# Half-block scores, outputs one pair late, and a split quadrant stretch in a fused attention and FFN kernel

## The chip, the cores and the metric

The kernel runs on one core of a Trainium2 chip. The metric is the device time of one execution in microseconds (us), lower is better. Times of a kernel are given as the median of several runs. "Faster", "same" and "slower" are decided at 2%, with a 95% interval. The profile is that of one execution; its times count from the start of the span.

TensorE multiplies matrices, VectorE and ScalarE do elementwise work, GpSimd does little here, and SyncE issues the transfers. PSUM is the memory in which the kernel keeps TensorE's results, in tiles that it calls banks. A *record* is the trace's entry for one instruction. The *chain* is the work that ended last, followed back from the last instruction, at each step to what released it. In the lines shown, `sc` and `sckv` are scores (`sckv` with the k-v sums), `kv` k-v sums, `y` attention outputs, `h` and `o` FFN products, `qT` and `kT` transposed queries and keys, `cs` the running sum.

## The reference

Everything is fp32. A gated linear attention is followed by an FFN with a squared ReLU, over 4 x 768 = 3072 tokens:

```python
# q, k, v, alpha: (4 batches, 8 heads, 768 tokens, 48)
for t in range(S):
    state = alpha[:, :, t, :, None] * state + np.einsum('bhd,bhe->bhde', k[:, :, t], v[:, :, t])
    y[:, :, t] = np.einsum('bhd,bhde->bhe', q[:, :, t], state)
x = y.transpose(0, 2, 1, 3).reshape(B * S, H * D)        # 3072 x 384
h = np.maximum(x @ w_in, 0.0)                            # w_in 384 x 2048
return h * h @ w_out                                     # w_out 2048 x 384
```

## The kernel before

The sequence is cut into 24 blocks of 128 tokens (6 chunks of 4 batches). The tokens' gates become a running sum of logarithms, so that inside a block attention is a masked matrix product: scores of all keys against all queries, times v, plus the queries times the state that the earlier blocks left. The FFN works on groups of four blocks (512 tokens) and uses a Strassen-like scheme of seven products for the groups after the first. While TensorE works on the FFN of one group, the attention of the next group is woven between the FFN's products.

The heads are 48 wide and fill only a quarter of the 128 x 128 array, so the attention products outside the opening run in quadrants of 64 x 64, four at a time. An fp32 product leaves two records in the trace, and each has a weight load beside it. Attention handles two blocks at a time, a *pair*. A *stretch* is a run of quadrant products with no FFN product between.

Before, the scores of a head had 128 + 64 columns: the first half of the keys against all queries, the second half against the second half of the queries.

```python
def sc(n):                                   # scores of one block
    ...
    for x in range(2):
        for i in range(2):                   # half of the keys
            for p in (x, NP // 2 + x):
                for e in range(2):
                    t = slice(64 * i, C)     # queries from that half on
                    nc.tensor.matmul(out=chunks(...), lhsT=ks[rows, p, 64 * i : 64 * (i + 1)],
                                     rhs=qs[rows, p, t], ...)

def y(n):                                    # outputs and k-v sums of a pair
    ... # state products
    for phase in range(2):
        ... # inner products with v, half of the rows in each phase
        pass_on("y")                         # GpSimd no-operation that orders the row groups
        ... # k-v sums of both blocks, half of the rows
        pass_on("kv")

PLAN = (                                     # when in the FFN each step of a pair is issued
    ...
    (5.0, "mq0 mq1 mk1"),                    # queries and keys times the gates (VectorE)
    ...
    (10.0, "sc0 sc1 am0"), (11.0, "am1"),    # stretch 1: scores of both blocks; masks
    (12.0, "y0 ev0 st0 st1"),                # stretch 2: y and k-v sums; copies; states
)
```

(Cut.) The two phases keep quadrants of different rows from writing one PSUM bank at the same time; the prediction below names the page behind this, and no run here tests it.

## Time and profile before

Median 575.7 us of 3 runs (575.4 to 576.33). The profiled execution has a span of 573.2 us.

| engine | busy, us | share |
|---|---|---|
| TensorE | 560.3 | 98% |
| VectorE | 327.6 | 57% |
| ScalarE | 222.8 | 39% |
| GpSimd | 4.5 | 1% |

Read it as follows. TensorE is the bound, and after the opening no wait of it is listed, so the time can only fall if TensorE gets less to do. That is the change's aim. The prediction below shows the lines of the page and of the chain.

### The profile page before, as it was taken

Reading aid. Unit: us, or ns where it says so; the run is one execution under the profiler, and the core shown is the slowest. Engines: PE = TensorE matmul, PEld = TensorE weight load, DVE = VectorE, ACT = ScalarE, POOL = GpSimd, SP = SyncE. Lnnn points to the kernel's source line nnn. Section 1 sums busy time; section 2 is a strip of 40 time slices with the busy share of each in tenths; the row PEclk is TensorE's granted clock in tenths of the full one; section 3 lists DMA queues with packets and bytes.
Section 4 is the critical chain, followed back from the end, with each engine's and each line's share of the span. In section 5 each row is a group of like instructions: output and inputs, shape, how many; then the busy total and the mean of one; then the engine's idle time right before and its main releaser. Section 6 shows DMA issues by size and latency. Waiting matters only on the chain.

```text
span 573.2 us, 11429 instructions
## 1 busy us (share of the span) xinstructions
PE 560.3 (98%) x4756; PEld 481.0 (84%) x4756; DVE 327.6 (57%) x653; ACT 222.8 (39%) x493; POOL 4.5 (1%) x29
## 2 busy tenths in 40 slices
PE   8789999999999999999999999999999999999996
PEld 6654565668889999889999888999988999988996
DVE  4988669875874534664534565652566443366430
ACT  4459865432344323334343234242333432333100
POOL 3000000000000000000000000000000000000000
PEclk9999999999999999999999999999999999999999
DMA  9986557621003335000454000435200340100001
GB/s 166 251 187 188 147 126 248 125 42 56 1 1 56 72 56 125 1 0 16 79 91 98 29 0 2 84 57 102 67 1 1 61 65 1 56 1 1 1 1 55
DMA packets 127963, 38.94 MB, mean 68 GB/s; under 512 B 119700, under 2 KB 122792, under 8 KB 127912
## 3 DMA queue, kind: packets, MB, share of 16 engines
q1 hardware_dynamic: 127912, 38.22, 30.5%
q8 instruction: 37, 0.61, 0.5%
q14 instruction: 14, 0.11, 0.1%
HBM read 33.45 MB, written 4.75 MB: 67 GB/s over the span
## 4 chain that ended last, share of the span: by engine, by line
PE 96%; DVE 2%; DMA 1%; issue 0%; ACT 0%; SPq 0%; POOL 0%; POOLq 0%
PE h L649 33%; PE o L720 32%; PE o L686 7%; PE h L611 7%; PE y L416 5%; PE cs L260 3%; PE sc L349 3%; PE qT L303 2%; PE kT L303 2%; PE kv L490 1%; DMA raw<-in_moe_w_in_dram 1%; PE warm L232 1%; PE sc L335 0%; DVE xT L514 0%; PE kv L393 0%
## 5 line engine op out<-in xcount | busy, mean ns | idle before, releaser
L649 PE MATMUL h<-xT,w_in 128*128 128x256 f32 x480 | 124.0, 379 | 0.0
L649 PEld LDWEIGHTS h<-xT,w_in 128*128 128x128 f32 x480 | 91.1, 190 | 12.3
L720 PE MATMUL o<-w_out,hid 128*128 128x192 f32 x480 | 83.3, 327 | 0.0
L720 PEld LDWEIGHTS o<-w_out,hid 128*128 128x128 f32 x480 | 78.7, 190 | 3.7
L514 ACT COPY xT<-y 32x256 f32<-32x256 f32 (+2 forms) x132 | 46.2, 364 | 77.1 <-PE y L416 73.5
L662 DVE TENSOR_TENSOR hid<-h,u 128x256 f32<-128x256 f32 x120 | 50.8, 424 | 28.9 <-PE h L649 25.0
L667 ACT ACTIVATE hid<-hid 128x256 f32<-128x256 f32 x40 | 16.7, 417 | 114.6 <-DVE hid L662 114.6
L662 DVE TENSOR_TENSOR u<-h,u 128x256 f32<-128x256 f32 x80 | 33.8, 423 | 35.3 <-PE h L649 22.9
L649 PE MATMUL h<-s3x,ws 128*128 128x256 f32 x160 | 47.6, 379 | 0.0
L611 PE MATMUL h<-xT,w_in 128*128 128x512 f32 (+1 forms) x108 | 43.6, 550 | 3.3 <-ACT xT L514 1.8
L384 DVE COPY_PREDICATED am<-parts,sc 128x384 f32<-128x384 uint32 x40 | 20.6, 577 | 45.7 <-PE sc L349 45.6
L686 PE MATMUL o<-w_out,hid 128*128 128x384 f32 x128 | 42.9, 489 | 0.0
L720 PE MATMUL o<-t,s 128*128 128x192 f32 x240 | 42.4, 328 | 0.0
L649 PE MATMUL h<-s3x,w_in 128*128 128x256 f32 x160 | 41.1, 379 | 0.0
L720 PEld LDWEIGHTS o<-t,s 128*128 128x128 f32 x240 | 39.0, 190 | 1.3
L611 PEld LDWEIGHTS h<-xT,w_in 128*128 128x128 f32 x108 | 19.8, 190 | 22.4 <-issue 16.3
L686 PEld LDWEIGHTS o<-w_out,hid 128*128 128x128 f32 x128 | 23.9, 190 | 15.6
L649 PEld LDWEIGHTS h<-s3x,ws 128*128 128x128 f32 x160 | 30.4, 190 | 4.1
L649 PEld LDWEIGHTS h<-s3x,w_in 128*128 128x128 f32 x160 | 30.4, 190 | 4.1
L720 PE MATMUL o<-t,hid 128*128 128x192 f32 x160 | 27.9, 329 | 0.0
L669 DVE SCALAR_TENSOR_TENSOR hid<-hid 128x512 f32<-128x512 f32 x40 | 27.2, 681 | 0.0
L720 PEld LDWEIGHTS o<-t,hid 128*128 128x128 f32 x160 | 25.8, 190 | 0.3
(109 smaller groups left out, 759.2 us busy)
## 6 DMA issues: line engine op xcount, KB each, us to landing
raw<-in_moe_w_in_dram SPq DMA_DIRECT2D x8, 768.0 KB, 5.5
raw<-in_moe_w_out_dram SPq DMA_DIRECT2D x8, 768.0 KB, 4.6
k_in<-in_k_dram SPq DMA_DIRECT2D x24, 192.0 KB, 5.0
out_dram<-osb SPq DMA_DIRECT2D x24, 192.0 KB, 2.1
v_in<-in_v_dram SPq DMA_DIRECT2D x23, 192.0 KB, 5.0
a_in<-in_alpha_dram SPq DMA_DIRECT2D x22, 192.0 KB, 3.6
q_in<-in_q_dram SPq DMA_DIRECT2D x22, 192.0 KB, 3.9
vx_in<-in_v_dram SPq DMA_DIRECT2D x40, 48.0 KB, 2.5
```

The lines of the kernel that those rows point to most:

```text
L260: nc.tensor.matmul(out=ps.rearrange("a p t -> a (p t)")[:, 0 : H * D], lhsT=causal, rhs=blk[n].pop("la"), start=True, stop=True,)
L303: nc.tensor.transpose(out=ps[:, p, :], in_=rows[:, 128 * p : 128 * (p + 1)], identity=ident)
L349: nc.tensor.matmul(out=chunks(ps[e].rearrange("a p t -> a (p t)"), half, p, i), lhsT=ks[rows, p, 64 * i : 64 * (i + 1)], rhs=qs[rows, p, t ...
L384: nc.vector.copy_predicated(out=o, mask=mask.unsqueeze(1).to_broadcast(list(o.shape)), data=data)
L416: ins = nc.tensor.matmul(out=slot(ps)[64 * half : 64 * half + D + G * e, t], lhsT=lhsT, rhs=rhs, start=key not in seen, stop=True, skip_gr ...
L514: copy(out=x[to : to + m, kk, t : t + 2], in_=blk[n]["y"][e][r : r + m, :, p // 2],)
L611: nc.tensor.matmul(out=ps, lhsT=w[:, kk, c0 : c0 + 128], rhs=xT[g][:, kk, cols], start=(kk == 0), stop=(kk == KM - 1),)
L649: nc.tensor.matmul(out=ps, lhsT=a, rhs=b, start=(step.isupper() and i == 0), stop=(i == len(pairs) - 1), skip_group_check=True,)
L662: nc.vector.tensor_tensor(out=o, in0=ps, in1=z, op=ALU.add)
L669: nc.vector.scalar_tensor_tensor(out=h2, in0=h2, scalar=0.0, in1=h2, op0=ALU.max, op1=ALU.mult)
L686: nc.tensor.matmul(out=acc[t][:, 0:DM], lhsT=hid[i][:, j, t * C : (t + 1) * C], rhs=w_out[i][:, j, :], start=(i == 0 and j == 0), stop=(i ...
L720: nc.tensor.matmul(out=acc[k][:, t, :], lhsT=lhs[:, j, t * C : (t + 1) * C], rhs=rhs[:, j, :], start=(first and r + j + t == 0), stop=(r = ...
```

## The change

The intent is to spend less TensorE time on the attention of each pair:

* A block is cut into two halves of 64. Each half only sees itself (scores of 64 + 64 columns), and the first half reaches the second through an intermediate state `u` = state + the first half's k-v sum.
* y runs one pair behind the scores. The quadrant work of a pair stands in two stretches, `ga` and `gb`, with one FFN product between: `ga` has scores and k-v sums of one block, and the state products and half the inner products of the pair before; `gb` has the other half of these, and scores and sums of the second block.
* Because of that a third pair is prepared beside the first FFN group.
* The second copy of v goes; the memsets of the masked scores move from VectorE to GpSimd; buffers are re-cut.
* In the opening, three products of zeros fill a hole of TensorE.

```diff
+    HALF = [slice(0, 64), slice(64, C)]
+    def scores(n):
+        for p in range(NP):
+            for h in range(2):
+                for e in range(2):
+                    nc.tensor.matmul(
+                        out=ps[e][HALF[h], 0, p, :], lhsT=ks[rows, p, HALF[h]],
+                        rhs=qs[rows, p, HALF[h]], start=True, stop=True, skip_group_check=True,
+                    )
+    def sums_copied(n):
+        u = blk[n]["u"] = ...
+        nc.vector.tensor_tensor(out=u, in0=ps[0][:, 1], in1=s_t[n % B], op=ALU.add)
...
+    def ga(a, n):
+        if n is not None:
+            for f in (scores, state_sums, masked, sums_copied):
+                f(n)
+        if a is not None:
+            ...  # state products: "s" for the first half, "u" for the second
+            for m, p, e in heads(a):
+                end = inner(product, m, p, e, e)
+            passed = nc.gpsimd.nop(nofuse=True)
+            dep(passed, end)
+        ...
+    def gb(a, n):
+        if a is not None:
+            for i, (m, p, e) in enumerate(heads(a)):
+                begin = inner(product, m, p, e, 1 - e)
+                if i == 0:
+                    dep(begin, passed)
+        if n is not None:
+            for f in (scores, state_sums, masked, sums_copied, next_state):
+                f(n + 1)
+        if a is not None:
+            ev(a)
...
-        (5.0, "mq0 mq1 mk1"),
...
-        (10.0, "sc0 sc1 am0"),
-        (11.0, "am1"),
-        (12.0, "y0 ev0 st0 st1"),
+        (4.5, "mq0 mk1 bl1"),
+        (5.0, "mq1"),
...
+        (9.5, "ga"),
+        (10.5, "gb"),
...
-        weights1 y0 cs3 ev0 br1 kT2 qT2 ei3 kc2 qc2 kv1 ...
+        weights1 y0 cs3 ev0 br1 kT2 qT2 zeros2 ei3 kc2 qc2 kv1 ...
...
-    events += attention(1, (2.0, 27.0), 2.1)
+    events += attention([(0, GB, False), (13.5, GB + 2, True), (27.5, GB + 4, True)], 2.35)
```

(Cut to the core.)

## The prediction

> **What bounds the kernel now.** I read the page's busy times first, then the chain that ended last in order of time, then the stretches and waits of TensorE.
>
> ```profile
> PE 560.3 (98%) x4756; PEld 481.0 (84%) x4756; DVE 327.6 (57%) x653; ACT 222.8 (39%) x493; POOL 4.5 (1%) x29
> ...
> PE 96%; DVE 2%; DMA 1%; issue 0%; ACT 0%; SPq 0%; POOL 0%; POOLq 0%
> ```
>
> TensorE is busy for 98% of the span and makes up 96% of the chain. The stretches say where the missing 13 us are: busy 29.9 of the first 38 us, 36.4 of the last 40.7, and in between practically everything. So after the opening only one thing shortens the program: less time in TensorE's own queue. The chain in order of time shows what one pair of attention blocks costs there (columns: start us, length us, what, records):
>
> ```profile
> 183.69 2.60 PE o L720 x16
> 186.30 1.50 PE sc L349 x64
> 187.79 2.80 PE o L720 x16
> 190.59 1.70 PE y L416 x63
> 192.29 0.47 PE kv L490 x32
> 192.76 0.66 PE y L416 x32
> 193.42 0.47 PE kv L490 x32
> 193.89 2.80 PE o L720 x16
> ```
>
> This pair takes 1.50 + 1.70 + 0.47 + 0.66 + 0.47 = 4.80 us in quadrants of the array (64x64 and smaller operands, four at a time). The FFN products around it show the cost of changing over: 16 records take 2.60 us in the middle of FFN and 2.80 after a quadrant stretch, so 0.20 us on the way out.
>
> Every fp32 product leaves two records. Counted in rounds of four records, one for each quadrant, kv gives the price of 64 moving columns: 32 records are 8 rounds in 0.47 us, 58 ns a round. The single records' start times inside y give 109 ns for a round of 128 columns and 55.5 for one of 64. Check: the second piece of y is 4 rounds of each, 4 x 109 + 4 x 56 = 0.66 us, as shown. The scores are 8 of each, 1.32 us; the chain has 1.50, so going in costs about 0.18. The first y piece is 12 x 109 + 4 x 56 = 1.53 us against 1.70, so 0.17. A pair therefore costs 4.80 + 2 x 0.20 = 5.20 us. The last chunk has no kv and its two pairs wait for the GpSimd nop that orders the row groups:
>
> ```profile
> 458.86 1.50 PE sc L349 x64
> ...
> 463.16 1.73 PE y L416 x63
> 464.98 0.89 PE y L416 x24
> ```
>
> That is 1.50 + 1.73 + 0.89 plus a gap of 0.09, with the changes 4.61 us. (Some records are missing; the times count.) All ten pairs outside the opening: 8 x 5.20 + 2 x 4.61 = 50.8 us.
>
> **What the Trainium skill says.** "TensorE: Matmul & The Clock Gate", section Back-to-back issue gap (and the part before it on the 56 ns gap), gives N/2.4 + 2.5 ns for a warm matmul and a start-to-start floor of about 25 ns however small it is. The first agrees: 2 x 128/2.4 + 2.5 = 109 ns. The floor doesn't hold for kv as recorded: 0.47 us / 32 = 14.7 ns. It does if only whole products count (29 ns). "TensorEngine Tiling (Array Packing)", Key Properties, says that changing the tiling mode drains TensorE: that is the 0.17 in and 0.20 out measured here. The same page, Gotcha 1, says that different row tiles can't write one PSUM bank at the same time; that is why each half of y has its own phase, and why the change puts FFN between them. The clock gate page, Part 1, puts the half clock after about 3.4 us of idle.
>
> **The change part by part.**
>
> *Half scores.* Before, the scores of a head and block are 128 + 64 columns (first half of the keys against all queries, second half against the second half), and so are the products with v. Now each half of 64 sees itself only, 64 + 64 columns, and the influence of the first half on the second goes through an intermediate state (the first half's k-v sum added to the state). Scores for a pair: 16 heads x 2 halves x 2 records / 4 = 16 rounds of 64. Inner products with v: 16 rounds. State products: 16 heads x 128 columns as before, but as 16 rounds of 64 columns, because the two halves use different states. kv: 16 rounds as before. Sum 64 rounds. At 57 ns (between the 55.5 and 58 above) that is 3.65 us, against 4.43 us of rounds now (scores 1.32, state 0.87, inner 1.32, kv 0.93). About 0.8 us a pair.
>
> *Two stretches.* The first takes the scores, k-v sums of one block and the state and half the inner products of the pair before (40 rounds, 160 records), the second the other half and the other block (24 rounds). Both pay 0.37 us of changing. y runs one pair late, so an eleventh pair of stretches closes the sequence: 22 x 0.37 = 8.1 us instead of 20 x 0.37 = 7.4.
>
> *Last chunk.* The change needs the first half's k-v sum there too, which before had none. It uses one row group only, two records at a time, 16 short rounds where other pairs have 16 full ones: still 64 rounds. These two pairs gain almost nothing.
>
> *Sum.* 10 x 3.65 + 8.1 = 44.6 us against 50.8: 6.2 us gained. With 58 ns a round 5.6, with 56 ns 6.9.
>
> *Vector work.* Before, a pair has 4 masks of 384 elements (577 ns), 4 adds of 128 (283) and 2 products of 256 (425): 4.29 us. After: 4 masks of 256, estimated 432 ns from the 577 for 384 and 722 for 512 elements, and 6 operations of 256 at 425: 4.28 us. Neutral, and off the path. Two memsets of 0.91 us leave VectorE for GpSimd, which is idle. The second copy of v (40 transfers of 48 KB) goes; DMA isn't on the path after the opening.
>
> *Zeros.* Three 256-column products of zeros fill the hole before the second kv of the opening. They need 6 x 216 ns (a 256-column record in the FFN) = 1.3 us; the hole is 1.77 us and ends with a VectorE copy. So they delay nothing. They also gain nothing: the opening's scores take 1.16 us for 16 records before and after the hole, so the clock never fell, as a hole of half the skill's 3.4 us suggests. The rest of the opening keeps its order.
>
> **The rivals.**
>
> *Short records are fed too slowly.* The longest run of 64-column records today is 32 (kv), and TensorE's queue is 64 deep by the skill, which holds 32 loads and 32 products: the 14.7 ns may be a drained buffer. Now 160 come in a row. The trace bounds it loosely: the 160 records of y and kv together take 3.30 us, 20.6 ns each, so after 32 buffered ones feeding keeps up with 3.30 us / 128 = 26 ns, no better shown. At 20 ns a record behind the buffer the first stretch would take 0.47 + 128 x 20 ns = 3.0 instead of 2.3 us, the second 1.75 instead of 1.4: 1 us a pair, and the time is about 580. At 25 ns about 590. Against it: kv's rounds stay at 58 ns to the last, also the second time, with only 0.66 us of longer records between.
>
> *The conversion of the weights becomes the bound.* Three pairs are prepared beside the first FFN group instead of two, and there ScalarE and VectorE are nearly full:
>
> ```profile
> core 0: us, PE busy (x) PEld busy (x) DVE busy (x) ACT busy (x) POOL busy (x), PEclk, DMA share, GB/s
> ...
> 43.00:48.00 5.00, 5.00 (x13) 2.28 (x12) 4.04 (x6) 4.94 (x9) 0.00 (x0) 1.00 0.89 234
> 48.00:53.00 5.00, 5.00 (x14) 2.38 (x13) 4.28 (x6) 4.94 (x9) 0.00 (x0) 1.00 0.77 290
> 53.00:58.00 5.00, 5.00 (x13) 2.18 (x12) 4.70 (x9) 4.94 (x10) 0.00 (x0) 1.00 0.20 31
> 58.00:63.00 5.00, 5.00 (x16) 2.43 (x15) 4.08 (x7) 4.42 (x8) 0.00 (x0) 1.00 0.51 166
> ```
>
> By the orders of the engines about 2.8 us more of ScalarE work (logarithms, exponentials of the second pair) fall in the 36 us of the first FFN product, where it idles about 6. Tightest: w_out's second slice is ready at 87.1 us and TensorE comes to it at 87.9, now. In the new order I put it ready at 85 to 86 and used at 88. A stall of 1 to 2 us is possible, more isn't likely: 571 to 572.
>
> *PSUM banks.* The second stretch's scores reuse the banks of the first, which VectorE must have read (masks, sum, state: five operations, some 1.7 us until the banks are free). From the first stretch's sums to those scores lie 1.4 us of y, 1.3 us of FFN, the changes and 0.5 us of inner products: 3.5 us. Covered unless VectorE is late; a wait of 0.3 us a pair would cost 3 us, 573.
>
> *Larger gain.* TensorE's 6 us are all it could give up: no pair waits today. So more than 2% (11.5 us) has no source.
>
> **Range and chances.** 575.7 - 6.2 = 569.5; I add 0.7 for small stalls of the second and third rival: 570.2. The low end, 567.3, takes cheaper rounds (56 ns) and changes of mode that cost less; the high end, 574.5, takes 0.4 us a pair lost to feeding or banks. Faster by over 2% (below 564.2): 3%. Within 2%: 93%. Slower (above 587.2): 4%, the feed limit.
>
> **What would show it.** Scores and k-v sums at about 0.47 us for 32 records in the chain, the y piece of the first stretch at 1.4 us for 96, the second stretch at 1.4 to 1.6; FFN after each still 0.20 longer. A gain of some 0.8 us a pair from the second FFN group to the fourth, none in the last chunk. TensorE gapless from 40 us on. First FFN phase about 3 us longer, since a third preparation moves in. Wrong would be: records over 18 ns apart in the long stretch (feed), TensorE waiting for VectorE's masks or sums at a stretch (banks), for w_in, w_out or relu in the first group (conversion), or an opening that ends elsewhere than at 38 us.

## The result, and the profile after

The changed kernel takes 572.68 us (median of 3 runs, 572.27 to 573.46) against 575.7. The ratio is 0.9948, interval 0.9925 to 0.997: "same" by the 2% rule, and the interval lies below 1. Ratios here are the mean time of one kernel's fast runs over the mean of the other's fast runs of the same rounds, so not quite the ratio of the medians quoted. The time lies inside the predicted range and 2.5 us above the predicted 570.2.

First the busy times and the chain of the page:

```profile
PE 558.4 (98%) x5146; PEld 477.7 (84%) x5146; DVE 327.2 (57%) x655; ACT 221.7 (39%) x493; POOL 5.8 (1%) x28
...
PE 93%; DVE 2%; DMA 2%; issue 1%; SPq 0%; ACT 0%; DVEq 0%
```

TensorE has more records (5146 for 4756) and is still the bound. It makes up less of the chain, and "issue", time for which the profile shows no cause, comes up from 0% to 1%.

The chain in order of time around one pair (start us, length us, what, records):

```profile
192.88 0.62 PE sckv L404 x32
193.50 0.47 PE sckv L430 x32
193.97 1.40 PE y L380 x90
195.37 1.50 PE o L712 x8
196.86 0.62 PE y L380 x31
197.49 0.47 PE sckv L404 x32
197.96 0.47 PE sckv L430 x32
```

This is the intended picture: scores 0.62 and 0.47 us, k-v sums 0.47, y 1.40 and 0.62. The pair takes 2.49 + 1.56 = 4.05 us in two stretches, for 4.80 before. The FFN piece between is 1.50 us for 8 records instead of 1.30, the 0.20 of changing out.

Taking for every stretch the time from its first record to the next FFN product, plus 0.20 for changing out: before, 20 stretches, 46.8 + 4.0 = 50.8 us. After, 22 stretches, at the lengths that a pair without holes has, 40.7 + 4.4 = 45.1 us. So 5.7 us are gained in the quadrants. But the end of TensorE's work moves by much less. The waits of TensorE from 40 us on, in the kernel after (who waits for whom: us in total, times, longest); before, the same question has no answer line at all:

```profile
PE qT L291 <- DVE q_in L266: 0.9, 1, 0.9
PE sckv L430 <- issue: 0.8, 2, 0.5
```

The first is a transposition of queries that waits for VectorE's multiplication of them. It stands alone at 84 us: 1.17 us pass from the start of the record before to the start of this one, where 0.11 us are usual, so some 1.1 us are lost. The second are holes in the second stretches, with no releaser. One of them in the chain:

```profile
287.22 0.47 PE sckv L404 x32
287.68 0.35 PE sckv L430 x23
288.03 0.54 issue
288.57 0.38 PE sckv L430 x9
```

After 23 of 32 records of the k-v sums TensorE stops for 0.54 us and then goes on with the same kind of record. Together the stretches of this execution are 1.7 us longer than the sum of 40.7.

Finally the profiled execution fell into a half clock once. The 5 us windows (busy time and records of each engine, then the granted clock, DMA share and GB/s):

```profile
core 0: us, PE busy (x) PEld busy (x) DVE busy (x) ACT busy (x) POOL busy (x), PEclk, DMA share, GB/s
...
35.00:40.00 5.00, 4.81 (x18) 3.85 (x18) 4.28 (x8) 2.00 (x6) 0.00 (x0) 0.66 1.02 327
```

So 572.68 is 5.7 us less in quadrants, and given back: 1.1 us of one wait, 1 to 2 us of holes, and in some executions about 1 us of clock. The experiments test each.

### The profile page after: what moved, and what is told of

Read it like the earlier page. It is cut to its first block, busy times and chain, and to the rows that moved or that the text cites. A ratio compares the mean times of both kernels' runs of the same rounds, so it can differ in the third digit from the quotient of the medians.

```text
span 571.5 us, 12168 instructions
## 1 busy us (share of the span) xinstructions
PE 558.4 (98%) x5146; PEld 477.7 (84%) x5146; DVE 327.2 (57%) x655; ACT 221.7 (39%) x493; POOL 5.8 (1%) x28
## 4 chain that ended last, share of the span: by engine, by line
PE 93%; DVE 2%; DMA 2%; issue 1%; SPq 0%; ACT 0%; DVEq 0%
PE h L641 33%; PE o L712 32%; PE o L678 7%; PE h L603 7%; PE y L380 4%; PE cs L248 2%; PE sckv L404 2%; PE qT L291 2%; PE sckv L430 2%; PE kT L291 2%; DMA raw<-in_moe_w_in_dram 1%; DMA a_in<-in_alpha_dram 1%; PE kv L350 0%; PE sc L333 0%; SPq L114 0%
## 5 line engine op out<-in xcount | busy, mean ns | idle before, releaser
L712 PE MATMUL o<-w_out,hid 128*128 128x192 f32 x480 | 81.9, 326 | 0.0
L414 DVE COPY_PREDICATED am<-halves_mask,sckv 128x256 f32<-128x256 uint32 x40 | 15.5, 441 | 57.2 <-PE sckv L430 57.2
L603 PE MATMUL h<-xT,w_in 128*128 128x512 f32 (+1 forms) x108 | 45.5, 569 | 2.6 <-ACT xT L520 1.8
```

The source lines that it names most:

```text
L414: nc.vector.copy_predicated(out=am_h(n)[:, e, n % 2], data=ps[e][:, 0], mask=halves_mask.bitcast(U32).unsqueeze(1).to_broadcast([128, NP, ...
L603: nc.tensor.matmul(out=ps, lhsT=w[:, kk, c0 : c0 + 128], rhs=xT[g][:, kk, cols], start=(kk == 0), stop=(kk == KM - 1),)
L712: nc.tensor.matmul(out=acc[k][:, t, :], lhsT=lhs[:, j, t * C : (t + 1) * C], rhs=rhs[:, j, :], start=(first and r + j + t == 0), stop=(r = ...
```

## The experiments

There were twelve runs, in four batches, each batch on another chip. The kernel before was run in each: medians 576.17 (13 runs), 575.69 (17), 575.45 (15), 575.71 (12). All runs below were correct and ran in the fast state.

The theory was, in three parts: (1) the wait at 84 us is an order of VectorE's own queue; (2) the holes are waits for the next piece of TensorE's instruction stream; (3) the zeros change nothing, the half clock is chance. Rivals: the holes are waits for PSUM banks or for VectorE's masks; the wait at 84 us is hidden behind another one and gains nothing when removed; the zeros guard the clock.

### The changed kernel again

No edit.

> The changed kernel unaltered, to settle its gain with more rounds. My accounting of its first trace: quadrant work of the ten pairs 45.2 us against 50.8 (gain 5.6), less 1.2 us where TensorE waits for the second scaled q of the second pair near 84 us, less 1.4 us in three holes inside dense quadrant stretches that end 1.41 to 1.44 us after a 16 KB instruction fetch lands, less some 0.5 us of a later first weight transfer. Expected 572.3 to 573.0, ratio 0.994 to 0.996. Rival (the clock): the profiled run also ran about 3.5 us at half clock near 35 us; if all runs do, the mean clock is 0.997 in each; if it is the phase of the clock's window, most runs show 0.999 to 1.000 and only a few are 1 us or more slower.

Measured: 572.03 us (571.45 to 573.31, 6 runs), ratio 0.9928 (0.9907 to 0.995). This profile has no half clock, so it is the one to compare with before. Stage by stage, from TensorE's first record of each stage to that of the next:

| stage, us | before | after (this run) | query multiplication early |
|---|---|---|---|
| start to first product of FFN group 1 | 132.1 | 137.5 | 136.8 |
| group 1 | 90.9 | 89.5 | 89.4 |
| group 2 | 90.9 | 90.4 | 90.0 |
| group 3 | 90.9 | 89.5 | 89.3 |
| group 4 | 89.7 | 84.4 | 84.4 |
| rest, to TensorE's last record | 74.6 | 74.6 | 74.6 |
| TensorE's last record | 568.9 | 565.8 | 564.4 |

The sum closes. A pair costs 0.75 us less, so groups 1 and 3 should be 1.5 us shorter and are 1.4 and 1.3 shorter; group 2, with two holes, is only 0.4 shorter. In the first row a third preparation moves in (some 3 us), the quadrants there are 6 stretches instead of 4 (10.3 + 1.2 against 9.6 + 0.8 us, so 1.1 more), and the wait of 1.1 us comes on top: 5.2 expected, 5.4 measured. Group 4 gives back the preparation: it is 5.3 shorter, of which 2.3 are its quadrants, so 3.0. In all: -5.7 in quadrants, +1.4 by which the stretches exceed 40.7 in this run, +1.1 of the wait, makes -3.2, and TensorE's end moved by -3.1.

The same two holes stood here, at the same records:

```profile
286.18 0.35 PE sckv L430 x23
286.53 0.30 issue
286.83 0.38 PE sckv L430 x9
```

### Without the zeros

```diff
-        weights1 y0 cs3 ev0 br1 kT2 qT2 zeros2 ei3 kc2 ...
+        weights1 y0 cs3 ev0 br1 kT2 qT2 ei3 kc2 ...
```

> The changed kernel without the zero products. Theory (zeros do nothing): same time within 0.3 us, and no half clock that the unaltered kernel doesn't also show. Rival (they keep the clock up): some or all runs lose 1 us or more with a mean clock of 0.997 or less, from slow records after the hole at 18 us. Their removal also shifts TensorE's instruction stream by 12 instructions, so the holes in the dense stretches should stay at the same multiples of 256 instructions counted in the new stream, 12 instructions later in the old one.

Measured: 572.29 us (571.57 to 575.77, 8 runs), ratio 0.9936 (0.9913 to 0.9958). The median is that of the kernel with zeros. But one run, the profiled one, took 575.77 us at a mean clock of 0.988, and its windows show why:

```profile
20.00:25.00 5.00, 5.00 (x35) 4.40 (x35) 4.12 (x8) 3.25 (x7) 0.00 (x0) 0.61 0.83 203
25.00:30.00 5.00, 5.00 (x27) 4.34 (x27) 4.75 (x9) 0.44 (x1) 0.00 (x0) 0.50 1.14 268
```

Right behind the hole at 18 to 20 us, which the zeros otherwise fill, the granted clock fell to half, for about 10 us in all (a window at 0.61 is at half for 3.9 of its 5 us, the next for all 5, the one after at 0.87 for 1.3). There the 16 records of a block's scores take 2.08 us, in the kernel before 1.16. So the hole can cost the clock. It rarely does, hence the unchanged median.

This run also tells something about the holes in the dense stretches that it wasn't made for. It has 12 TensorE records less in front of them (3 products, two records each, with a weight load each). Counting TensorE's records from 0 at the start of the trace, that is products, loads and its sequencer's own instructions (72 of them in the whole program), the hole stands at record 5313 in both runs. In the work, however, it has moved by 6 product records, from after the 23rd to after the 29th of the same group:

```profile
290.09 0.47 PE sckv L430 x29
290.56 0.20 issue
290.75 0.33 PE sckv L430 x3
```

So the hole belongs to a place in the instruction stream and not to a place in the work. A bank or a mask that is late would hold the same product.

### The query multiplication early

```diff
-        (4.5, "mq0 mk1 bl1"),
-        (5.0, "mq1"),
+        (4.5, "mq0 mq1 mk1 bl1"),
```

> The second q of a pair is scaled together with the first one, so in VectorE's order before the masks of the second stretch in the first FFN group. Theory (VectorE's order costs 1.2 us at 84 us): TensorE no longer waits at the second transposition of q, time 1.0 to 1.2 us below the unaltered kernel. Rival (VectorE is simply late there, or the wait moves to the next operand): less than 0.4 us gained, and TensorE waits for k, the masks or w_out instead.

Measured: 570.74 us (570.4 to 571.92, 6 runs), ratio 0.9909 (0.9886 to 0.9933), 1.3 us below the changed kernel on the same chip. The wait of the transposition is gone from the list of waits, which now holds only one line:

```profile
PE sckv L430 <- issue: 0.3, 1, 0.3
```

So part (1) is shown: in the changed order, VectorE came to the second block's queries only after the masks, sums and states of `gb`, and TensorE waited. The kernel was run again under three other labels below, with medians of 571.02, 571.03 and 571.44, on other chips; so the gain over 572.03 is 1.3 us on the same chip and 0.6 to 1.0 across chips, about the 1.1 us of the wait. The rival had a small part in it: in this profile TensorE gains 1.1 us at 84 us, but at 90 us it starts a transposition of keys 0.2 us later, behind a copy by ScalarE. As its opening, which the edit doesn't touch, also ran 0.2 us later, the first row of the table is only 0.7 shorter.

### One stretch instead of two

```diff
-        (9.5, "ga"),
-        (10.5, "gb"),
+        (9.5, "ga gb"),
```

> Both stretches of a pair without FFN between them. If only the changes of tiling counted: 11 x 0.37 = 4 us faster than the unaltered kernel. Theory: it is not faster but slower or equal, because (a) the second scores wait for VectorE to release their banks, about 0.5 us a pair, (b) the ordering through GpSimd is bare, about 0.3 us a pair, and (c) 512 TensorE instructions come in about 3.7 us, while each block of 256 takes about 1 us to fetch and 1.4 us until it is used: at least one hole of 0.3 to 1.5 us in most pairs, each ending 1.4 us after a fetch. Expected 571 to 576. Without (c) the holes would all have a VectorE or GpSimd releaser and the time would be 572 or less.

Measured: 581.4 us (580.88 to 584.16, 5 runs), ratio 1.0099 (1.0071 to 1.0126), 9.4 us above the changed kernel, though its 11 stretches instead of 22 change the tiling eleven times less. In the chain of the same pair two things take the place of the FFN product between the stretches:

```profile
196.71 0.03 POOLq L485
196.73 0.04 issue
196.78 0.65 PE y L380 x26
197.42 1.27 issue
```

The GpSimd no-operation that orders the row groups is now waited for: from 196.42 to 196.78 between records, 0.36 us, and 0.34 to 0.36 in each of the ten stretches that have it. Then a hole of 1.27 us. In this kernel eight such holes stand in the stretches, at records 1473, 2241, 3265, 4033, 5313, 7105, 7873 and 8897, and a ninth right behind a stretch at 6081. Each of these numbers is 193 plus a multiple of 256. The trace's transfers show an instruction stream arriving in 40 pieces of 16 KB (queue, packets, MB, share of the DMA engines' time):

```profile
q8 instruction: 40, 0.66, 0.5%
```

TensorE has 10365 records, 259 for each piece, so 256 a piece fits. Each of the eight holes ends 1.24 to 1.61 us after such a piece has landed, the ninth 1.66 us.

The expected time, 571 to 576, was missed, though points (b) and (c) came: the nine holes make some 9.6 us and the ten waits for the no-operation 3.4, less 11 x 0.37 = 4.1 us of changing, so 8.9 of the 9.4 us. The waits for banks, point (a), did not come. TensorE's waits from 40 us on:

```profile
PE sckv L404 <- issue: 2.2, 3, 0.8
PE y L380 <- issue: 2.1, 3, 1.3
PE sckv L430 <- issue: 2.0, 2, 1.1
PE o L712 <- issue: 1.5, 1, 1.5
PE o L678 <- DVE w_out L178: 0.5, 1, 0.5
PE qT L291 <- DVE q_in L266: 0.3, 1, 0.3
```

The first four lines are the nine holes, without a releaser; the last two are waits for a weight and for queries in the first group.

### Instructions shifted by no-operations (two runs)

```diff
+        if g == 1 and j < 4:
+            for _ in range(2):          # 4 in the second run
+                nc.tensor.nop(nofuse=True)
```

> The kernel with the query multiplication early, plus 56 TensorE no-operations spread over the first half of the first group's FFN-in stage, so that every later instruction stands 56 places further on in the program. Theory (the holes of 0.3 to 0.8 us in the dense stretches after 200 us are waits for the next 16 KB piece of the instruction stream): the hole that stood at 285.6 us vanishes or moves by 56 instructions of the program, away from the matmul it stood at; whatever hole is left stands at a whole number of 256 instructions and ends 1.3 to 1.6 us after a piece has landed. Rival (the holes belong to the place in the program: a bank, a mask or an eviction there): the hole stays at the same matmul. Time: the no-operations cost what 56 issue slots cost, 0 to 1.5 us; holes give back or take 0 to 1.5 us: 569.5 to 572.5.

> The same with 112 no-operations, so another position of the piece boundaries. Theory: again holes only at whole multiples of 256 instructions, at other matmuls than with 56 or none, each ending 1.3 to 1.6 us after a piece has landed; between 0 and 3 holes in all. Rival: the same matmuls as before. Time 569.5 to 573.5.

Measured: 571.02 us (570.32 to 571.74, 4 runs), ratio 0.9914 (0.9901 to 0.9928), and 571.03 (570.75 to 571.62, 5 runs), ratio 0.9916 (0.9902 to 0.9929). As a test these failed. The holes stood at records 6081 and 5313, again 193 plus multiples of 256, where a program with 56 or 112 more instructions should have them at 137 or 81. The starts of the pieces' transfers stand at the same record counts as without the no-operations, to the end of the program (the last but one at 9895 and 9897, without them at 9897). So nothing was shifted; most likely the no-operations never reached TensorE's program, but no record shows what became of them. The runs count as repeats of the kernel before this one.

### Zeros in both holes of the opening

```diff
+        for _ in range(3 if j == 0 and cols.start else 0):      # before the second half of the first FFN block
+            nc.tensor.matmul(out=ps[:, 0:256], lhsT=s[:, 0:128], rhs=s, start=True, stop=True)
```

> The kernel with the query multiplication early, plus three more products of the zeros tile before the first block's second half, in the wait of 3 us for weights at 32 to 35 us of the opening. Theory (the opening's waits now and then cost the granted clock for some microseconds, and products of zeros in a wait keep it): no run at a clock of 0.993 or less, none over 1.5 us above the median; the median the same within 0.4 us of 570.7. Rival (the dips have another cause and come at random): as many dips as without, the median the same. If the three products are late and stand in front of needed work: up to 0.7 us slower.

Measured: 570.86 us (570.56 to 571.21, 4 runs), ratio 0.9912 (0.9898 to 0.9925). The four runs have clocks of 0.999 to 1.0. The median is unchanged, as both expected. It also shifts the instruction stream by 12 records, this time for real, and the hole stood at record 6081 again, 1.30 us after a piece had landed.

### The kernel before with the zeros alone

```diff
-        weights1 y0 cs3 ev0 br1 kT2 qT2 ei3 kc2 ...
+        weights1 y0 cs3 ev0 br1 kT2 qT2 zeros2 ei3 kc2 ...
```

> The kernel before with the three products of zeros alone, in the hole at 18 to 20 us. The zeros fill a wait, so the median should be as before, 575.7 to 576.2. Theory (they guard against a granted clock of 0.99 and its 2 to 3 us): none of its runs is over 1.5 us above its median, while the kernel before shows such runs in about one of five. Rival (they gain nothing, as the prediction had it): outliers as often as before.

Measured: 575.53 us (575.15 to 576.48, 13 runs), ratio 0.9997 (0.9989 to 1.0005). The zeros cost nothing. None of the 13 runs is slow, but in this batch the kernel before had no slow run either (17 runs, at most 576.49), so the batch alone doesn't decide. Over all batches it does. Without zeros, 11 of 65 runs had a mean clock of 0.993 or less (10 of 57 of the kernel before, each at 578 us or more, and 1 of 8 of the changed kernel without them). With zeros it was none of 75 (13 + 3 + 6 + 6 + 5 + 9 + 4 + 6 + 6 + 10 + 7, all kernels here that have them); the lowest was 0.995. Batch by batch, without zeros it was 4 of 21, 0 of 17, 3 of 15 and 4 of 12, so the rate differs from batch to batch; with zeros it was none in any. So zeros spare about one execution in six some 2.8 us. That all eleven lost it at this one hole isn't shown: only one of them was profiled.

### Unaltered beside the next two

The kernel with the query multiplication early.

> The kernel with the query multiplication early, unaltered, to stand beside the next two on the same chip: 570.4 to 571.7, median 570.9, one or two holes of 0.3 to 0.6 us in the second stretches after 280 us, each ending 1.3 to 1.6 us after a 16 KB piece of the instruction stream has landed.

Measured: 571.44 us (571.23 to 572.61, 6 runs), ratio 0.9927 (0.9908 to 0.9947). Three small holes, 0.28 to 0.29 us between the starts of records, one more than expected and one of them already at 195 us, at records 3265, 6081 and 7105, ending 1.42 to 1.50 us after a piece. The same program thus has its holes at other boundaries from run to run (5313 in the first run of it), but at boundaries only.

### Two FFN products between the stretches

```diff
-                    w = t + at * scale
+                    w = t + at * scale + (f == "gb" and scale == 1)
...
-            events = attention([(0, n, True), (13.5, n + 2, True)], 1) + ...
+            events = attention([(0, n, True), (12.5, n + 2, True)], 1) + ...
```

> The same with two FFN products instead of one between the two stretches of a pair from the second group on (and the second pair of a group one product earlier). Theory (a hole comes where 256 TensorE records pass in less than some 3.4 us, which is when the boundaries of two pieces lie one in each stretch of a pair with 1.3 us of FFN between): now 256 records across the two stretches take at least 4.7 us, so no hole is left after 140 us in the profile and the median is 0.4 to 0.8 us below the unaltered one: 570.2. Rival (the holes come from VectorE's masks and sums holding the banks of the second stretch, or from something else in it): against banks the longer FFN would help as well, but the holes' ends would not stand 1.4 us after a piece landed; against anything else they stay. If the later end of the last pair of a group delays the sums of x for the next group: up to 1 us slower a group.

Measured: 572.26 us (571.25 to 572.58, 6 runs), ratio 0.9935 (0.9916 to 0.9954). The expectation was missed twice. There is no gain, and a hole is left:

```profile
305.64 1.05 PE y L380 x69
306.69 0.87 issue
307.56 0.58 PE y L380 x23
```

It stands at record 5825, 1.38 us after a piece landed, so it is of the same kind. What I had left out is that the first stretch alone has 320 records. Record 5569, the boundary before, was passed at 304.60, just after that stretch began, so both boundaries lay in one stretch. The next piece's transfer started at 305.26. The holes between the two stretches did go, as the theory said. The higher median has another source: the profiled run has a clock of 0.66 in the window at 35 to 40 us, behind the second hole of the opening, and four of the six runs have mean clocks of 0.997, at 572.0 to 572.6 us. The other two took 571.25 and 571.79.

### Three stretches

```diff
+    def gc(a, n):        # scores and sums of the second block, taken out of gb
...
         (10.5, "gb"),
+        (11.5, "gc"),
```

> The same with three stretches a pair: the inner products that close y, and the scores and sums of the second block, each in a stretch of its own with an FFN product between. Theory: a stretch costs 0.37 us of changing the tiling (0.17 in, 0.20 out); nine pairs get one more, 3.3 us; no hole is left, 0.5 us back: 573.2 to 574.0, median 573.6. In the chain both new stretches show the 0.15 us longer first piece and the FFN product after each is 0.20 longer. Rival (one more stretch costs less because part of the change was paid inside the long stretch anyway): below 572. Rival (banks freed earlier or later matter more than the changes): a wait appears before the third stretch, above 575.

Measured: 573.28 us (572.7 to 574.83, 10 runs), ratio 0.9956 (0.9938 to 0.9975), 1.8 us above the unaltered one beside it. No hole is left. The chain:

```profile
195.71 0.62 PE y L380 x31
196.34 1.50 PE o L715 x8
197.83 0.62 PE sckv L404 x32
```

The scores that took 0.47 us inside the stretch take 0.62 at the head of their own, and another FFN piece is 1.50 us instead of 1.30. All stretches together are 1.3 us longer than the hole-free 40.7, plus 9 x 0.20 for changing out: 3.1 us for nine stretches, 0.35 each. That is the 0.37 of the prediction, within its rounding. The unaltered run's stretches exceed 40.7 by 1.4 us, which this kernel saves, so 1.7 us more in all, and 1.8 was measured.

### All together, with even stretches

Query multiplication early, zeros twice, two FFN products between, and the first half of the inner products moved to the head of `gb`, so that both stretches have 256 records:

```diff
     def gb(a, n):
+        if n is not None:
+            if a is not None:
+                inner_first(a)                   # moved from ga
+            for f in (scores, state_sums, masked, sums_copied, next_state):
+                f(n + 1)
         if a is not None:
             ... # second half of the inner products, then ev(a)
```

> The best of what the runs gave, put together: query multiplication early, zeros in both holes of the opening, two FFN products between the stretches, and the stretches made even, 256 TensorE records each instead of 320 and 192 (the first half of the inner products moves from the first stretch to the head of the second, the scores and sums of the second block stand between the two halves of the inner products and cover the GpSimd no-operation). Theory (a hole needs two boundaries of instruction pieces within 3.1 to 3.9 us of TensorE's time): two boundaries no longer fit inside one stretch, except that one may stand in the first few records and the next just behind the stretch; so no hole, or one, of at most 1 us, after 140 us. Zeros keep the clock: every run at 0.998 or more. Median 570.3, between 569.9 and 571.0. Rival (the new order puts the masks of the second block or the end of y later and VectorE or ScalarE then keep TensorE waiting): a wait in front of a stretch or of the next group's products, 571.5 to 573.

Measured: 573.08 us (572.77 to 573.95, 7 runs), ratio 0.9937 (0.9912 to 0.9961). No hole is left in the stretches, which together fell to 40.5 us. Six of seven runs have clocks of 0.999 or 1.0; one has 0.996, with its dip before 17 us, where there are no zeros. But the rival came true. TensorE now waits once in each of groups 1 to 3, with 1.27 us from start to start where 0.16 is usual:

```profile
PE cs L248 <- ACT a_in L243: 2.8, 3, 0.9
PE h L613 <- DVE w_in L178: 0.6, 1, 0.6
```

The second line is the last wait of the opening, which the kernel before has too (0.62 us, at 38 us). The second pair's running sum waits for ScalarE's logarithm of its gates. That logarithm stands in ScalarE's queue behind the copies of y, which start later now that y ends the stretch, while the second pair begins one product earlier; no run tests which of the two counts. Without these three waits the time would be 573.08 - 3 x 1.11 = 569.8 us; that is an estimate, and such a version was not run.

The best that was run is the changed kernel with the query multiplication early (570.74, and 571.02 to 571.44 in its repeats) or, with the same median and steadier, that with zeros twice (570.86). Both beat both original kernels.

## Why the prediction was right or wrong

**The size was right for the most part.** 570.2 was predicted, 572.7 and 572.0 came, inside the range and the class; of the 5.5 us forecast as a gain, 3.0 and 4.1 came. That the range held is in part luck: its upper end stood for losses to feeding and banks, and the losses that came were others. The prediction's sum had two terms, 6.2 us of quadrant time and 0.7 of small stalls.

* *Half scores* held. 64 rounds a pair were predicted at 57 ns. The pair's 4.05 us less two changes in of 0.17 are 3.71 us, 58 ns a round. The prediction's own alternative of 58 ns gave 5.6 us; 5.7 was measured. So this term was mis-sized by 0.5 us, by the choice of 57.
* *Two stretches* held: 0.35 us each, measured with a third one, against 0.37.
* *The gain per stage* held: some 0.8 us a pair was predicted for the groups in the middle; a pair's stretches are 0.75 shorter, groups 1 and 3 are 1.4 and 1.3 shorter for two pairs, and group 2 only 0.4, with its two holes. The first phase was to be 3 us longer and is 5.4. The preparation was counted, but not that the first phase holds six stretches instead of four (1.1), nor the wait (1.1).
* *Vector work neutral* held: 327.6 us before, 327.2 after. *Banks* held: no wait for a bank appeared in any list of TensorE's waits after the opening.

**"TensorE gapless from 40 us on" failed**, and with it the term of 0.7 us for stalls, which measured 2.5 in the undisturbed profile (1.1 + 1.4).

* *Conversion.* The rival looked for TensorE waiting for weights, and allowed 1 to 2 us. 1.1 came, but from the queries: VectorE's order put their multiplication behind the second stretch's masks and sums. Moving it forward took the wait away.
* *Feed.* The rival asked whether each short record is fed fast enough and would have seen records over 18 ns apart. They are not: 32 take 0.47 us everywhere. The limit was one level up: the instructions themselves come in pieces of 256, and the dense stretches use a piece up before the next is there. Before, the shortest time between two boundaries was 3.7 us; after, several lie 3.4 us apart and some 1.8 to 2.2. A piece took 0.4 to 1.8 us from the boundary before it to the start of its transfer in these stretches, 0.9 to 1.6 to land and, at the holes, about 1.4 until its first instruction ran. (Where two boundaries lay only 1.9 or 2.1 us apart in the changed kernel, the second piece had been started 1.4 to 2.0 us before the first boundary, and no hole came.) I argued from k-v rounds that stay at 58 ns to the last, which says nothing of a supply that fails only every 256 records.

That the holes are such waits rests on 23 holes after the opening (over 0.2 us from start to start, inside stretches, without the waits for the GpSimd no-operation and the first record of a stretch) in ten runs: every one at 193 plus a multiple of 256, ending 1.24 to 1.61 us after a piece landed, the same number staying while the work under it moved by 6 products. And in none of the 14 traces is a piece used sooner than 1.24 us after it landed, with a hole or without; in the kernel before never sooner than 3.1, in the last kernel, which has no hole, never sooner than 2.1. That 1.4 us pass between landing and use is only read from the trace; what happens in them stays open.

**"They also gain nothing: the clock never fell" was wrong for the zeros.** It was read from one execution. That the zeros delay nothing was right. But without zeros about one execution in six loses clock (in the only one of them that was profiled, right behind this hole), and a median hides it. Part (3) of my theory after the result fell with this, too.

## What to carry to other kernels

When a change makes TensorE's records shorter, count records per microsecond as well as microseconds: a stretch that runs 256 of them in less than about 3.5 us can outrun its instruction stream. One FFN product between two stretches was worth its change of tiling here (without it 9.4 us slower), a second cut was not (1.8 us slower). Moving work into an earlier phase moves its place in the queues of the other engines, so check for every operand what stands in front of it there. And look at the slowest runs before calling a guard useless: one profile can't show a thing that happens one time in six.

## What the Trainium skill lacked or had wrong

* "Trainium Architecture — The Big Picture", section The software stack, has the instruction streams brought to the engines when the program is loaded. In the trace they keep arriving while it runs: 40 pieces of 16 KB in the changed kernel, 37 before. "Runtime: NRT & Kernel Launch", section Instruction fetch mechanics, does have the blocks of 16 KiB and 256 instructions, fetched while the program runs, and calls the cost of crossing into the next one mostly hidden. The size agrees; the cost isn't hidden in dense stretches: 23 holes, of 0.3 to 1.5 us from start to start. I found no page with a piece's 0.9 to 1.8 us of transfer or the 1.2 us and more until it is used.
* "TensorE: Matmul & The Clock Gate", Part 1, gives an idle window of about 3.4 us for the half clock. In the profiled run without zeros a hole of 1.8 us, with other gaps near it, was enough: TensorE was busy for 3.04 of the 5 us before the clock fell. It isn't always enough: the profile of the kernel before has the same 3.04 us and keeps its clock, and 11 of 65 runs lost clock.
* "TensorEngine Tiling (Array Packing)", Key Properties, speaks of the drain at a change of tiling mode without a price. Here it is 0.35 us for going in and out once (nine more stretches, 3.1 us).
